# Sliding-window attention for one decoded token: another order of the steps between two units

## The chip, the cores and the metric

The kernel runs on one core of a Trainium2 chip. The metric is device time in microseconds of one execution; the time before is the median of three runs. All data are fp32.

## The reference, cut to what matters

```python
xn = layernorm(x)                                   # x [2, 1, 512]
q = (xn @ wq) -> [2, 32 heads, 128]                 # 8 key/value heads, 4 query heads share one
k, v = last 4096 rows of k_cache, v_cache           # [2, 8, 32768, 128] each
p = softmax(q @ k.T * 128**-0.5)                    # over the 4096 rows
s = (p @ v).reshape(2, 1, 4096) @ wo                # wo [4096, 512]
g = silu(gmlp(xn))                                  # w_in [512, 1792], w_out [896, 512]
out = x + s * g
```

The windows of keys and of values are 33.5 MB each, and each is read once; the weights are 22 MB.

## The kernel before, in words

**Units.** One unit is two key/value heads of one batch row: 4096 rows of keys and of values for each, 4.19 MB each way. There are eight units, four for each batch row. The keys of a unit lie in a slot as 64 blocks (J) of 128 partitions by 128, a half of the partitions for each head. They are worked on in four quarters (NCH) of 16 blocks.

**Steps of a unit.** Each is a function; the tile names are those of the profile.

- `turn(u, m)`: DVE turns quarter m of the keys within blocks of 32 by 32, `kt<-k`. Two buffers.
- `shares(u, m)`: PE multiplies the turned quarter by the queries, four column groups side by side, `sh<-kt,qbd` into one PSUM bank that all quarters share; ACT copies it out, `shs<-sh`. Two buffers for shs.
- `add_shares(u, m)`: PE adds the four partial sums over the head dimension, `s<-shs,add_dq`, into bank m of the score tile `s`. That tile has four banks and there is one of it for all units.
- `row_max`: DVE takes maxima of s, `m<-s`. `share_max`: small DVE steps `t` and `mg`, a PE product `mo<-mg,same` that spreads the maxima over the partitions, then `mx` and the exponent's bias `nb`.
- `probs`: ACT takes the exponent of all scores, `p<-s,nb`, with row sums `l`, in two instructions. `probs_t`: DVE turns p in two halves, `pT<-p`. `weights`: PE `mo<-l,heads` and the small DVE steps `ls` and `wd`, which make the scale.
- `values`: PE multiplies pT by the values, `acc<-v,pT`, 16 products that the profile shows as 32 matmuls. `scale_out`: ACT scales them, `o<-acc,wd`, four instructions. `collect`: PE puts o into the batch row's bank, `col<-o,sel`; for the last unit of a batch row DVE then reduces that bank to `oT`.

**Order.** PE, DVE, ACT and SP are wrapped so that each engine runs its instructions in the order in which the program issues them (`InOrder`, line 37: nearly every row of the profile has this line, and tiles tell the steps apart). The order of the loop body is therefore the order on each engine. What an instruction waits for is found from the tiles that it reads and writes.

**Loads.** SP issues all large loads: w_in, w_out, two halves of wq, then keys and values, then wo in pieces. They share four slots of 4.19 MB (`ring`); a load waits until the last reader of the slot that it takes is done, and all later loads wait behind it on SP. The order is k0, k1, v0, k2, v1, ..., k7, v6, v7. Readers that free a slot are the last turn of a unit's keys and the last product of its values.

**Before and behind the units.** A first stage makes the layer norm, the gMLP gate and the queries. Behind the units PE multiplies oT by wo (`part`, `so`), and the gate and x are applied.

Of the kernel before, what the change touches and what calls it, by code (L numbers as in the profile page):

```python
# [11 lines left out]
ALU = mybir.AluOpType  # L12
AX = mybir.AxisListType
# [8 lines left out]
def ap(t, offset, dims):  # L22

    return bass.AP(tensor=t.tensor, offset=t.offset + offset, ap=[list(t.ap[0])] + [list(d) for d in dims])
# [18 lines left out]
def kernel(  # L43
# [25 lines left out]
    NU = B * HKV // 2  # L69
    J = 2 * W // P  # L70
    JC = 512 // 32
    NCH = J // JC
# [7 lines left out]
    def slot(name):  # L80
        return ring.tile([P, SLOT], F32, tag="slot", name=name)
# [4 lines left out]
    def bank(name, tag):  # L86
        return ps.tile([P, 512], F32, tag=tag, name=name)
# [21 lines left out]
    def by_group(t, b, c0, c1):  # L109
        return bass.AP(tensor=t.tensor, offset=t.offset + b * D + c0, ap=[[DC, G], [1, c1 - c0]])  # L110

    def load_unit(cache, u, name):

        b, w = divmod(u, NU // B)
        t = slot(f"{name}{u}")
        first = cache[b, 2 * w, SK - W :, :]
        src = bass.AP(tensor=first.tensor, offset=first.offset, ap=[[SLOT, P // 2], [SK * DH, 2], [1, SLOT]])
        sp.dma_start(t, src)
        return t.rearrange("p (j d) -> p j d", d=DH)
# [163 lines left out]
    def q_of(u, dq):  # L283
        return ap(qbd, (u.n * 4 + dq) * 32, [[1, 32]])
# [5 lines left out]
    def turn(u, m):  # L290

        u.kt[m] = sb.tile([P, JC, DH], F32, tag="kt", name=f"kt{u.n}_{m}")
        dve.transpose(
            u.kt[m].rearrange("p j d -> p (j d)"), u.k[:, JC * m : JC * m + JC, :].rearrange("p j d -> p (j d)")
        )

    def shares(u, m):

        u.sh = bank(f"sh{u.n}_{m}", "sh")
        for dq in range(4):  # L300
            pe.matmul(
                u.sh[32 * dq : 32 * dq + 32, :], q_of(u, dq), u.kt[m][:, :, 32 * dq : 32 * dq + 32],
                start=True, stop=True,
            )
        u.shs[m] = sb.tile([P, 512], F32, tag="shs", name=f"shs{u.n}_{m}")
        act.activation(u.shs[m], u.sh, AF.Copy)

    def add_shares(u, m):
        if m == 0:
            u.s = ps.tile([P, NCH, 512], F32, tag="s", name=f"s{u.n}")  # L310
            u.m4 = sb.tile([P, 2, 2], F32, tag="m4", name=f"m4_{u.n}")
        pe.matmul(u.s[:, m, :], add_dq, u.shs[m], start=True, stop=True)

    def row_max(u, half):
        n = NCH // 2 * 512
        dve.tensor_reduce(
            u.m4[:, half, :], ap(u.s, half * n, [[1, 2], [2, n // 2]]), axis=AX.X, op=ALU.max
        )

    def share_max(u):  # L320
        t = sb.tile([P, 2], F32, tag="t", name=f"t{u.n}")
        dve.tensor_scalar_mul(t, u.m4[:, :, 0], am[:, 0:1])
        dve.scalar_tensor_tensor(t, u.m4[:, :, 1], am[:, 1:2], t, op0=ALU.mult, op1=ALU.add)
        mg = sb.tile([P, 2, G], F32, tag="mg", name=f"mg{u.n}")
        dve.tensor_mul(mg, ap(t, 0, [[1, 2], [0, G]]), ap(grpm, 0, [[0, 2], [1, G]]))
        u.mo = bank(f"mo{u.n}", "mo")
        pe.matmul(u.mo[:, : 2 * G], same, mg.rearrange("p a g -> p (a g)"), start=True, stop=True)
        mx = sb.tile([P, 1], F32, tag="mx", name=f"mx{u.n}")
        dve.reduce_max(mx, u.mo[:, : 2 * G], axis=AX.X)
        u.nb = sb.tile([P, 2], F32, tag="nb", name=f"nb{u.n}")  # L330
        dve.scalar_tensor_tensor(u.nb, ap(mx, 0, [[0, 2]]), -SCALE, negm, op0=ALU.mult, op1=ALU.add)

    def probs(u):

        u.p = sb.tile([P, J, 32], F32, tag="p", name=f"p{u.n}", bufs=1)
        u.l = sb.tile([P, 2], F32, tag="l", name=f"l{u.n}")
        for a in range(2):
            act.activation(
                ap(u.p, a, [[2, J * 16]]), ap(u.s, a, [[2, J * 16]]), AF.Exp,
                bias=u.nb[:, a : a + 1], scale=SCALE, accum_out=u.l[:, a : a + 1],  # L340
            )

    def probs_t(u, half):
        if half == 0:
            u.pT = sb.tile([P, J, 32], F32, tag="pT", name=f"pT{u.n}", bufs=1)
        h = slice(J // 2 * half, J // 2 * (half + 1))
        dve.transpose(u.pT[:, h].rearrange("p j r -> p (j r)"), u.p[:, h].rearrange("p j k -> p (j k)"))

    def weights(u):
        pe.matmul(u.mo[:, 2 * G : 2 * G + 2], heads, u.l, start=True, stop=True)  # L350
        l = sb.tile([P, 1], F32, tag="ls", name=f"ls{u.n}")
        dve.reduce_sum(l, u.mo[:, 2 * G : 2 * G + 2], axis=AX.X)
        dve.reciprocal(l, l)
        u.wd = sb.tile([P, 4], F32, tag="wd", name=f"wd{u.n}")
        dve.tensor_scalar_mul(u.wd, diag, l)

    def values(u):
        u.acc = bank(f"acc{u.n}", "acc")
        NQ = J // 4
        for q in range(NQ):  # L360
            c = q % G
            pe.matmul(
                u.acc[32 * c : 32 * c + 32, :], ap(u.pT, 4 * q * 32, [[4, 32]]),
                u.v[:, 4 * q : 4 * q + 4, :].rearrange("p j d -> p (j d)"), start=(q < G), stop=(q >= NQ - G),
            )

    def scale_out(u):
        u.o = sb.tile([P, 4, DH], F32, tag="o", name=f"o{u.n}")
        for jj in range(4):
            act.activation(  # L370
                u.o[:, jj, :], u.acc[:, jj * DH : (jj + 1) * DH], AF.Copy, scale=u.wd[:, jj : jj + 1]
            )
# [3 lines left out]
    def collect(u):  # L376
        if u.w == 0:
            col[u.b] = bank(f"col{u.b}", "col")[:, : 4 * 32].rearrange("p (j d) -> p j d", j=4)
        for e in range(4):
            pe.matmul(  # L380
                col[u.b][32 * u.w : 32 * u.w + 32], sel[:, 3 - e : 35 - e], u.o[:, :, 32 * e : 32 * e + 32],
                start=(e == 0), stop=(e == 3),
            )
        if u.w == NU // B - 1:
            dve.reduce_sum(oT[:, :, 16 * u.b], col[u.b].rearrange("p j d -> p d j"), axis=AX.X)

    units = []
    for n in range(NU):
        u = Unit()
# [1 line left out]
        u.b, u.w = divmod(n, NU // B)  # L391
        units.append(u)

    for n in range(NU + 1):
        if n < NU:
            units[n].k = load_unit(k_cache, n, "k")
        if n > 0:
            units[n - 1].v = load_unit(v_cache, n - 1, "v")

    wo_v = wo.rearrange("(p j) d -> p j d", j=32)  # L400
    blocks = []
# [2 lines left out]
    for i, piece in enumerate(pieces):  # L404
        t = slot(f"wo{i}").rearrange("p (j d) -> p j d", d=D)
        at = 0
        for n in piece:
# [3 lines left out]
            if j == 16:  # L411
                for b in range(B):
                    sp.dma_start(x4[16 * b : P : 32, :], by_group(x, b, 0, DC))

    prev = None
    for u in units:
        if prev is None:
            turn(u, 0)
            turn(u, 1)
        shares(u, 0)  # L420
        shares(u, 1)
        if prev is not None:
            scale_out(prev)
        add_shares(u, 0)
        turn(u, 2)
        shares(u, 2)
        add_shares(u, 1)
        turn(u, 3)
        shares(u, 3)
        add_shares(u, 2)  # L430
        if prev is not None:
            collect(prev)
        row_max(u, 0)
        add_shares(u, 3)
        row_max(u, 1)
        share_max(u)
        probs(u)
        nxt = units[u.n + 1] if u.n + 1 < NU else None
        if nxt is not None:
            turn(nxt, 0)  # L440
            turn(nxt, 1)
        probs_t(u, 0)
        probs_t(u, 1)
        weights(u)
        values(u)
        prev = u
    scale_out(prev)
    collect(prev)


    EARLY = 28
# [48 lines left out]
```

## Time and profile before

| | |
|---|---|
| three runs, median (lowest to highest) | 265.07 us (264.8 to 265.68) |
| the profiled execution, its own time | 264.93 us |
| its span in the profile | 263.1 us |
| busy PE / DVE / ACT / POOL | 160.1 / 136.1 / 54.8 / 2.5 us |
| granted TensorE clock, mean | 0.789 |
| DMA | 89.54 MB, mean 340 GB/s |

The span is what the trace covers; the profiled execution took 1.8 us more. All times inside a trace count from the span's start. A row of the view in order of time has the start in us, the duration, the engine, the line, the operation, out<-in by tile names, shapes and count, and in brackets the idle time before it and who ended it. Rows that follow closely are merged, so a row can stand for several instructions (x8). The page cuts the span into 40 slices; PEclk is the granted clock in tenths of full speed.

### The profile page before, as it was taken

Reading aid. Unit: us, or ns where it says so; the run is one execution under the profiler, and the core shown is the slowest. Engines: PE = TensorE matmul, PEld = TensorE weight load, DVE = VectorE, ACT = ScalarE, POOL = GpSimd, SP = SyncE. Lnnn points to the kernel's source line nnn. Section 1 sums busy time; section 2 is a strip of 40 time slices with the busy share of each in tenths; the row PEclk is TensorE's granted clock in tenths of the full one; section 3 lists DMA queues with packets and bytes.
Section 4 is the critical chain, followed back from the end, with each engine's and each line's share of the span. In section 5 each row is a group of like instructions: output and inputs, shape, how many; then the busy total and the mean of one; then the engine's idle time right before and its main releaser. Section 6 shows DMA issues by size and latency. Waiting matters only on the chain.

```text
span 263.1 us, 2303 instructions
## 1 busy us (share of the span) xinstructions
PE 160.1 (61%) x898; PEld 49.3 (19%) x898; DVE 136.1 (52%) x191; ACT 54.8 (21%) x109; POOL 2.5 (1%) x13
## 2 busy tenths in 40 slices
PE   0261893493299348926871884198438926872893
PEld 0111220021112112311221222122211212121141
DVE  3234116945916783576648364916692677545000
ACT  4014100020304111330313040305120430313100
POOL 3000000000000000000000000000000000000000
PEclk9996577577569858965995799569858975997698
DMA  7999999999999998997699399909992997591000
GB/s 280 427 450 438 438 412 453 408 438 433 428 446 408 463 408 354 453 399 323 239 418 458 162 398 399 473 5 398 403 466 90 418 458 323 209 376 53 0 2 1
DMA packets 3794, 89.54 MB, mean 340 GB/s; under 512 B 438, under 2 KB 454, under 8 KB 840
## 3 DMA queue, kind: packets, MB, share of 16 engines
q1 hardware_dynamic: 3768, 89.40, 80.6%
q8 instruction: 7, 0.11, 0.2%
q14 instruction: 3, 0.02, 0.0%
q10 hardware_dynamic: 16, 0.01, 0.0%
HBM read 89.40 MB, written 0.00 MB: 340 GB/s over the span
## 4 chain that ended last, share of the span: by engine, by line
PE 57%; DVE 31%; ACT 5%; DMA 4%; issue 2%; ACTq 0%; DVEq 0%
PE acc L37 17%; PE s L37 13%; PE sh L37 13%; DVE kt L37 13%; DVE m L37 7%; DMA win<-in_B_w_in_dram 4%; DVE pT L37 4%; PE q_ps L37 3%; PE part L37 2%; PE z L37 2%; ACT shs L37 2%; PE mo L37 2%; DVE t L37 1%; PE y L37 1%; ACT p L37 1%
## 5 line engine op out<-in xcount | busy, mean ns | idle before, releaser
L37 DVE STREAM_TRANSPOSE kt<-k 128x2048 f32<-128x2048 f32 x32 | 72.0, 2289 | 35.6 <-PE sh L37 35.6
L37 PE MATMUL acc<-v,pT 128*32 128x512 f32 x256 | 45.9, 880 | 18.0 <-DVE pT L37 18.0
L37 ACT ACTIVATE shs<-sh 128x512 f32<-128x512 f32 x32 | 19.1, 597 | 115.3 <-PE sh L37 115.3
L37 PE MATMUL sh<-kt,qbd 128*32 128x512 f32 x256 | 36.1, 639 | 10.3 <-ACT shs L37 6.2
L37 PE MATMUL s<-shs,add_dq 128*128 128x512 f32 x64 | 36.7, 656 | 5.6 <-DVE m L37 5.6
L37 DVE TENSOR_REDUCE m<-s 128x2 f32<-128x1024 f32 x16 | 19.6, 1224 | 29.3 <-PE s L37 29.3
L37 ACT ACTIVATE p<-s,nb 128x1024 f32<-128x1024 f32 x16 | 18.5, 1169 | 48.2 <-DVE nb L37 48.2
L37 DVE STREAM_TRANSPOSE pT<-p 128x1024 f32<-128x1024 f32 x16 | 18.7, 1205 | 2.5 <-ACT p L37 2.5
L37 PEld LDWEIGHTS acc<-v,pT 128*32 128x32 f32 x256 | 10.4, 158 | 46.8 <-issue 28.2
L37 PE MATMUL mo<-l,heads 128*128 128x2 f32 x16 | 4.7, 363 | 23.5 <-ACT p L37 23.5
L37 PEld LDWEIGHTS s<-shs,add_dq 128*128 128x128 f32 x64 | 9.7, 191 | 29.5 <-issue 29.5
L37 PE MATMUL mo<-mg,same 128*128 128x8 f32 x16 | 4.0, 321 | 16.3 <-DVE mg L37 16.3
L37 PEld LDWEIGHTS sh<-kt,qbd 128*32 128x32 f32 x256 | 5.8, 111 | 36.4 <-ACT shs L37 25.7
L37 ACT ACTIVATE o<-acc,wd 128x128 f32<-128x128 f32 x32 | 9.1, 373 | 7.5 <-PE acc L37 7.5
L37 PE MATMUL q_ps<-wq,xnT 128*32 128x512 f32 x64 | 9.3, 747 | 0.0
L37 PE MATMUL col<-o,sel 128*32 128x128 f32 x64 | 8.5, 276 | 1.3 <-ACT o L37 1.3
L37 PEld LDWEIGHTS mo<-l,heads 128*128 128x128 f32 x16 | 4.0, 311 | 24.2 <-ACT p L37 24.2
L37 PEld LDWEIGHTS col<-o,sel 128*32 128x32 f32 x64 | 6.3, 109 | 7.5 <-issue 5.3
L37 PEld LDWEIGHTS mo<-mg,same 128*128 128x128 f32 x16 | 3.2, 251 | 22.9 <-DVE mg L37 22.9
L37 PE MATMUL z<-win,xnT 128*32 128x448 f32 x32 | 4.8, 762 | 4.0 <-DMA win<-in_B_w_in_dram 4.0
L37 PE MATMUL part<-wo,oT 128*32 128x512 f32 x56 | 6.2, 593 | 0.4 <-issue 0.4
L37 PE MATMUL y<-wout,hT 128*32 128x512 f32 x14 | 3.6, 1059 | 4.0 <-DVE hT L37 4.0
(99 smaller groups left out, 57.8 us busy)
## 6 DMA issues: line engine op xcount, KB each, us to landing
k<-in_A_k_cache_dram SPq DMA_DIRECT2D x8, 4096.0 KB, 12.3
v<-in_A_v_cache_dram SPq DMA_DIRECT2D x8, 4096.0 KB, 18.0
wq<-in_A_wq_dram SPq DMA_DIRECT2D x2, 4096.0 KB, 29.4
wo<-in_A_wo_dram SPq DMA_DIRECT2D x1, 4096.0 KB
win<-in_B_w_in_dram SPq DMA_DIRECT2D x1, 3584.0 KB
wo<-in_A_wo_dram SPq DMA_DIRECT2D x1, 2048.0 KB
wout<-in_B_w_out_dram SPq DMA_DIRECT2D x1, 1792.0 KB, 15.0
wo<-in_A_wo_dram SPq DMA_DIRECT2D x1, 1024.0 KB
```

Of the source, the lines that this page charges most:

```text
L37: return self.tc.keep_in_program_order(call(*args, **kwargs))
```

## The change

The order of the loop body is written anew, and two other things go with it.

- Order. The exponent of the previous unit, `probs(prev)`, now opens the pass of a unit. Behind it come the turn and the shares of quarter 0, then the previous unit's `probs_t` and `weights`, the adding product of quarter 0, and the previous unit's `values`. Quarters 1 to 3 follow, each as turn, shares, add. Then come `scale_out` and `collect` of the previous unit, the maxima and `share_max`. The reduction to oT has its own step, `gather`, behind `share_max`.
- Maxima. The two instructions read quarters 0 to 2 and quarter 3, where they read two quarters each. Both stand behind the last `add_shares`.
- Loads. The order is k0, v0, k1, v1, ..., k7, v7.

```diff
-    def row_max(u, half):
-        n = NCH // 2 * 512
+    def row_max(u, i, c0, c1):
         dve.tensor_reduce(
-            u.m4[:, half, :], ap(u.s, half * n, [[1, 2], [2, n // 2]]), axis=AX.X, op=ALU.max
+            u.m4[:, i, :], ap(u.s, 512 * c0, [[1, 2], [2, 256 * (c1 - c0)]]), axis=AX.X, op=ALU.max
         )
...
+    def gather(u):
         if u.w == NU // B - 1:
             dve.reduce_sum(oT[:, :, 16 * u.b], col[u.b].rearrange("p j d -> p d j"), axis=AX.X)
...
-    for n in range(NU + 1):
-        if n < NU:
-            units[n].k = load_unit(k_cache, n, "k")
-        if n > 0:
-            units[n - 1].v = load_unit(v_cache, n - 1, "v")
+    for u in units:
+        u.k = load_unit(k_cache, u.n, "k")
+        u.v = load_unit(v_cache, u.n, "v")
...
+    def finish(u):
+        scale_out(u)
+        collect(u)
+
     prev = None
     for u in units:
-        if prev is None:
-            turn(u, 0)
-            turn(u, 1)
+        if prev is not None:
+            probs(prev)
+        turn(u, 0)
         shares(u, 0)
-        shares(u, 1)
         if prev is not None:
-            scale_out(prev)
+            probs_t(prev, 0)
+            probs_t(prev, 1)
+            weights(prev)
         add_shares(u, 0)
-        turn(u, 2)
-        shares(u, 2)
-        add_shares(u, 1)
-        turn(u, 3)
-        shares(u, 3)
-        add_shares(u, 2)
         if prev is not None:
-            collect(prev)
-        row_max(u, 0)
-        add_shares(u, 3)
-        row_max(u, 1)
+            values(prev)
+        for m in range(1, NCH):
+            turn(u, m)
+            shares(u, m)
+            add_shares(u, m)
+        if prev is not None:
+            finish(prev)
+        row_max(u, 0, 0, NCH - 1)
+        row_max(u, 1, NCH - 1, NCH)
         share_max(u)
-        probs(u)
-        nxt = units[u.n + 1] if u.n + 1 < NU else None
-        if nxt is not None:
-            turn(nxt, 0)
-            turn(nxt, 1)
-        probs_t(u, 0)
-        probs_t(u, 1)
-        weights(u)
-        values(u)
+        if prev is not None:
+            gather(prev)
         prev = u
-    scale_out(prev)
-    collect(prev)
+    probs(prev)
+    probs_t(prev, 0)
+    probs_t(prev, 1)
+    weights(prev)
+    values(prev)
+    finish(prev)
+    gather(prev)
```

## The prediction

> **What bounds the kernel now.** I read the page first (where the engines and the clock stand), then the order of time inside one unit, then the clock in small windows, then the instructions of the first unit.
>
> ```profile
> span 263.1 us, 2303 instructions
> ...
> PEclk9996577577569858965995799569858975997698
> ...
> GB/s 280 427 450 438 438 412 453 408 438 433 428 446 408 463 408 354 453 399 323 239 418 458 162 398 399 473 5 398 403 466 90 418 458 323 209 376 53 0 2 1
> ...
> PE 57%; DVE 31%; ACT 5%; DMA 4%; issue 2%; ACTq 0%; DVEq 0%
> ```
>
> A slice is 6.58 us. DMA carries 430 to 450 GB/s at first and then shows holes (162, 5, 90): from the middle on, loads wait for buffers. A unit brings 2 x 4.19 MB, 19.5 us at 430 GB/s. The chain of waits is PE and DVE in alternation. So what counts is the dependent chain of one unit. This is unit 2 with the end of unit 1, in the view in order of time:
>
> ```profile
> 101.91 1.03 PE L37 MATMUL sh<-kt,qbd 128*32 128x512 f32 x8
> 103.08 0.60 ACT L37 ACTIVATE shs<-sh 128x512 f32<-128x512 f32 x1 [9.89 <-PE sh L37]
> 103.72 1.06 PE L37 MATMUL sh<-kt,qbd 128*32 128x512 f32 x8 [0.79 <-ACT shs L37]
> 104.72 1.12 PE L37 MATMUL s<-shs,add_dq 128*128 128x512 f32 x2
> 104.92 0.60 ACT L37 ACTIVATE shs<-sh 128x512 f32<-128x512 f32 x1 [1.24 <-PE sh L37]
> 105.78 1.06 PE L37 MATMUL sh<-kt,qbd 128*32 128x512 f32 x8
> ...
> 108.82 1.13 PE L37 MATMUL s<-shs,add_dq 128*128 128x512 f32 x2
> 109.99 1.23 DVE L37 TENSOR_REDUCE m<-s 128x2 f32<-128x1024 f32 x1 [2.47 <-PE s L37]
> 111.36 1.10 PE L37 MATMUL s<-shs,add_dq 128*128 128x512 f32 x2 [0.42 <-DVE m L37]
> 112.49 1.22 DVE L37 TENSOR_REDUCE m<-s 128x2 f32<-128x1024 f32 x1 [1.28 <-PE s L37]
> 113.75 0.23 DVE L37 TENSOR_SCALAR t<-m,am 128x2 f32<-128x2 f32 x1
> ...
> 114.49 0.59 PE L37 MATMUL mo<-mg,same 128*128 128x8 f32 x2 [2.04 <-DVE mg L37]
> 115.33 0.16 DVE L37 SCALAR_TENSOR_TENSOR nb<-mx,negm 128x2 f32<-128x2 f32 x1
> 115.41 4.50 DVE L37 STREAM_TRANSPOSE kt<-k 128x2048 f32<-128x2048 f32 x2
> 115.58 1.18 ACT L37 ACTIVATE p<-s,nb 128x1024 f32<-128x1024 f32 x1 [5.96 <-DVE nb L37]
> 119.83 2.33 DVE L37 STREAM_TRANSPOSE pT<-p 128x1024 f32<-128x1024 f32 x2
> 121.08 5.35 PE L37 MATMUL acc<-v,pT 128*32 128x512 f32 x32 [2.46 <-DVE pT L37]
> 126.25 1.03 PE L37 MATMUL sh<-kt,qbd 128*32 128x512 f32 x8
> ```
>
> From one unit's first key product to the next is 24.34 us: 1.81 with an open copy (101.91 to 103.72), 6.16 for three pairs at 2.05 with the copy hidden, 3.87 for both maxima and the last adding product between them, 1.66 to the next turn, 4.42 for two turns, 1.25 for the first turned probabilities, 5.17 for the values. Two things are to be seen. The first maximum reads quarters 0 and 1 alone, yet starts when quarter 2 is added, and the last product waits for that maximum: waits go by the whole score tile, in program order. And PE is nearly idle from 112.5 to 121.1, which costs clock:
>
> ```profile
> 49.47:52.88 3.41, 2.69 (x16) 0.20 (x8) 3.41 (x2) 0.60 (x1) 0.00 (x0) 0.50 1.00 432
> 145.04:148.45 3.41, 3.02 (x16) 0.79 (x20) 1.90 (x5) 0.00 (x0) 0.00 (x0) 0.50 0.74 312
> 76.78:80.19 3.41, 2.62 (x25) 0.45 (x17) 1.76 (x1) 0.60 (x1) 0.00 (x0) 1.00 1.08 456
> 76.50:77.00 0.50, 0.50 (x8) 0.10 (x4) 0.00 (x0) 0.00 (x0) 0.00 (x0) 0.72 0.30 131
> 90.00:90.50 0.50, 0.30 (x2) 0.20 (x2) 0.17 (x1) 0.00 (x0) 0.00 (x0) 0.93 0.76 328
> 100.50:101.00 0.50, 0.50 (x8) 0.18 (x4) 0.00 (x0) 0.00 (x0) 0.00 (x0) 0.83 1.07 459
> ```
>
> (Busy windows: length, PE, PEld, DVE, ACT, POOL, granted clock, DMA.) A mean of 0.72, 0.93 and 0.83 over half a microsecond puts the changes of clock at 76.78, 90.43 and 100.67: 13.65 and 10.24 us apart, four and three steps of 3.41. PE goes up only behind a step that it filled: 3.02 of 3.41 busy was enough (the row from 145.04), 2.69 was not (from 49.47). At full clock a step with 2.62 busy stayed up (from 76.78). The Trainium skill, "TensorE: Matmul & The Clock Gate", Part 1, gives the same free-running window of 3.4 us with two rates; the trace agrees, with its 3.41.
>
> **The change, part by part.** Rows of the first unit, at half clock, and of one large group and one small:
>
> ```profile
> 46.32 6.70 DVE L37 STREAM_TRANSPOSE kt<-k 128x2048 f32<-128x2048 f32 x3
> 48.69 1.94 PE L37 MATMUL sh<-kt,qbd 128*32 128x512 f32 x8 [4.05 <-DVE kt L37]
> 50.69 0.60 ACT L37 ACTIVATE shs<-sh 128x512 f32<-128x512 f32 x1 [18.48 <-PE sh L37]
> 53.20 2.07 PE L37 MATMUL s<-shs,add_dq 128*128 128x512 f32 x2
> 63.70 0.23 DVE L37 TENSOR_SCALAR t<-m,am 128x2 f32<-128x2 f32 x1
> ...
> 96.29 5.79 PE L37 MATMUL acc<-v,pT 128*32 128x512 f32 x32 [2.46 <-DVE pT L37]
> 98.01 0.19 PEld L37 LDWEIGHTS acc<-v,pT 128*32 128x32 f32 x4 [0.66 <-issue]
> ...
> L37 DVE TENSOR_REDUCE oT<-col 128x32 f32<-128x128 f32 x2 | 0.6, 294 | 10.4 <-PE col L37 10.4
> ```
>
> *Quarters 1 to 3.* PE's order is now shares, add, shares, add of the same quarter, so each adding product waits for its own copy: 1.20 to the copy's start (103.72 to 104.92), 0.64 for the copy and its hand-over (103.08 to 103.72), 1.06 to the next product (104.72 to 105.78): 2.90 where 2.05 was. The turns (2.29 each) run ahead and are hidden. Two quarters, then 1.20 + 0.64 + 1.17 (108.82 to 109.99) up to the maximum: 8.81.
>
> *Maxima.* Both now stand behind the last adding product in program order, so by the whole-tile wait seen above the 3 + 1 split overlaps nothing. 1024 columns take 1.22 and 128 take 0.29, so 1.04 ns a column: 1.75 + 0.69 + 0.04 = 2.48 from the first to t. Scale-out and collect, now behind the last quarter, run beside the maxima on ACT and PE, which have nothing else until mo; were they longer than the 3.2 us that lie between, the rest would come on top.
>
> *Softmax.* t to the first turn stays 1.66 (113.75 to 115.41); turn to product 2.37 (46.32 to 48.69). The second turn and the turned probabilities, 2.2 + 1.25 on the old path, go behind the first product: p, two of 1.18, ends 0.3 after that product starts (115.58 + 2.4 against 115.41 + 2.37), and pT with its 2.33 ends 2.6 after it, before the adding product is through.
>
> *First quarter under the softmax.* It finds PE at half clock (idle from collect on for about 5 us): 2.00 to the copy (48.69 to 50.69), 0.65, 2.00 for the adding product (the 2.07 of the row at 53.20, less the overlap with the next): 4.65. The sums' small product (as long as the 0.59 at 114.49) fits into the copy's 0.65.
>
> *Values.* 32 matmuls in 8 groups of 0.85 (0.19 and 0.66 idle at 98.01) are 6.84 at half clock, 3.42 at full. If the clock rises w after the first product starts, a unit takes 8.81 + 2.48 + 1.66 + 2.37 + 4.65 + 3.42 + (w - 4.65)/2 = 23.39 + (w - 4.65)/2. Before, the stretch from 96.29 had its rise at 100.67 (w = 4.4); the shortest way is the 3.0 us of the row from 145.04, the longest two steps less the 0.39 us that may be missing, 6.4. So a unit takes 22.6 to 24.3 us. Seven steps are 23.9; a shorter unit moves its start forward against the steps, lengthens w and comes back to that. I take 23.85.
>
> *Loads.* v0 now goes second and k1 third, which enters its queue at the same place:
>
> ```profile
> 37.21 0.53 SPq L37 DMA_DIRECT2D v<-in_A_v_cache_dram  x1
> 77.32 1.03 PE L37 MATMUL sh<-kt,qbd 128*32 128x512 f32 x8
> 225.32 1.03 PE L37 MATMUL sh<-kt,qbd 128*32 128x512 f32 x8
> 237.17 0.23 DVE L37 TENSOR_SCALAR t<-m,am 128x2 f32<-128x2 f32 x1
> ```
>
> 26.5 MB stand in the queue up to its end; the slices reach that at about 64 us, and its turn is due near 69: hidden, 5 us to spare (each us beyond that costs one, once). Later keys wait for a unit's last turn, values for the value products, one after the other on SP; each is issued more than a unit's time before its use, and 19.5 us of transfer fit into 23.85.
>
> *First unit.* Its quarters now run at 4.65 cold. With copies open, a step holds about as little PE work as the one from 49.47 that did not raise the clock, so the rise comes a step later, at 59.7 instead of 56.3 (five and six steps ahead of 76.78): 4.65 + 4.65 + 3.7 + 3.0 = 16.0, then 2.48, so t stands at 67.2, not 63.7. The values then end near 79.6, where 77.32 stood: +2.3. All quarters cold would be 1.6 more; a rise one step earlier 1.7 less.
>
> *Sum.* 79.6 + 6 x 23.85 + 8.81 + 2.48 = 234.0 for the last unit's t, against 237.17; behind it the same steps follow. Before, the six units took (225.32 - 77.32)/6 = 24.67 each, of which one holds a gather. So -3.2 us: 264.93 in the profiled execution becomes 261.7. The median of the runs, 265.07, lies 0.14 above that execution; this is inside the rounding.
>
> **The rivals.**
> *The copy's gap keeps the clock down* (slower). Place: between the first product and its adding product, where only the small product of the sums runs. If that does not count as work, the step with the gap looks like the one of 2.69 of 3.41, and the rise waits for a step wholly behind the gap: w is 5.6 to 8.8, a unit 23.9 to 25.5, on average 24.7; with +2.3 at the start and -0.55 at the end (11.29 for 237.17 - 225.32) 267. It decides from a gap between 0.39 us (3.02 busy) and 0.72 (2.69). For it: the first unit's steps. Against it: 0.59 us of the small product stands in the gap.
> *The spaced quarters drop the clock.* Then each costs 4.65 and not 2.90, 5 us a unit, near 300. The row from 76.78 speaks against it: three quarters busy, clock 1.00. The Trainium skill, same page, "A second HAM failure mode: psum-queue depth-cycling", says that small idle times between groups of matmuls made the clock swing; that would give this case, and the trace so far does not bear it out.
> *No change.* Every open hand-over costs 0.2 us more than the rows (the adding product loads 128 columns of weights behind its wait, of which the trace shows no exposed case behind ACT): 0.8 a unit, and the gain is gone: 265.
> *The change does not do what it says, the good way:* the split maxima do overlap. Then 1.75 us of a unit goes, 250. The waits of the tile speak against it.
> *A lucky phase:* the first unit's clock rises a step earlier and the units stay below seven steps: 258.
>
> **How the numbers follow.** Forecast 0.64, with 259.8 to 263.5 as its own range; clock kept down 0.14; spaced quarters 0.03; no change 0.10; overlap 0.02; lucky phase 0.07. 0.3% (0.8 us) is about what a measurement of this kernel tells from no change. Faster: 0.64 + 0.02 + 0.07 and a third of the clock case where units stay near 23.9, 0.77. Same 0.09, slower 0.14. The range leaves out the overlap, the dropped clock, the worse half of the clock case and the better half of the lucky phase, 0.16 together; it takes the rest: 259.0 to 266.5.
>
> **What would show it.** In the changed profile: PE's idle before s with ACT shs as its releaser, about 0.7 each, four a unit; the quarters 2.9 apart; both maxima behind the last s, 1.75 and 0.69; the value products without a wait on pT; 23.9 us from unit to unit, and changes of the clock seven steps apart; k1's first turn waiting for nb, not for DMA. I am wrong if units take over 24.6, if the clock is 0.50 in quarters 1 to 3 of later units, or if the first maximum starts before the last s ends.

## The result, and the profile after

The changed kernel takes 262.41 us (median of 20 executions, 260.07 to 266.19), the kernel before 264.52 (20 executions beside them, 262.5 to 266.1). The ratio is 0.9874, 95% interval 0.9844 to 0.9904: 1.3% faster. The 20 executions of the changed kernel fall into two groups, 11 near 261 us and 9 near 265, and the ratio compares the first, to which the profiled execution (261.21 us) belongs, with all of the kernel before; the ratio of the plain medians is 0.992, and why the second group is longer was not profiled.

From the page after, the lines that answer to those of before: span, granted clock and DMA rate in 40 slices, and the chain that ended last by engine.

```profile
span 259.4 us, 2310 instructions
...
PEclk9996579569569967995998599779959995997798
...
GB/s 284 418 466 409 450 428 414 450 429 419 450 424 422 450 419 344 384 424 421 149 414 470 328 237 407 404 248 323 467 419 167 404 424 386 197 396 56 0 3 1
...
PE 53%; DVE 18%; DMA 16%; ACT 9%; issue 3%; ACTq 0%
```

The span is 3.7 us shorter, and the row of GB/s still has holes (149, 167): waiting work, not the loads, sets the end. On the chain DVE has gone from 31% to 18%, and ACT, the open copies, from 5% to 9%. DMA has gone from 4% to 16%, but nearly all of it lies before 47.02 us, where the chain now follows the load of k0 back; in the units no load is on it. The groups say the same of DVE and ACT (busy us, mean ns of one, then PE's idle time ahead of them and its releaser):

```profile
L37 PE MATMUL s<-shs,add_dq 128*128 128x512 f32 x64 | 43.6, 768 | 21.3 <-ACT shs L37 21.3
...
L37 PE MATMUL acc<-v,pT 128*32 128x512 f32 x256 | 35.8, 709 | 0.7 <-DVE pT L37 0.7
```

The wait on pT, which the product of values had in every unit before (2.46 in the rows shown), is gone but for 0.7 in the last unit. In its place the adding products wait 21.3 us for their copies. One unit in the order of time:

```profile
102.95 1.03 PE L37 MATMUL sh<-kt,qbd 128*32 128x512 f32 x8
104.77 1.13 PE L37 MATMUL s<-shs,add_dq 128*128 128x512 f32 x2 [0.79 <-ACT shs L37]
...
107.67 1.12 PE L37 MATMUL s<-shs,add_dq 128*128 128x512 f32 x2 [0.78 <-ACT shs L37]
...
110.56 1.12 PE L37 MATMUL s<-shs,add_dq 128*128 128x512 f32 x2 [0.78 <-ACT shs L37]
...
111.73 2.36 DVE L37 TENSOR_REDUCE m<-s 128x2 f32<-128x1536 f32 x2 [5.36 <-PE s L37]
114.12 0.23 DVE L37 TENSOR_SCALAR t<-m,am 128x2 f32<-128x2 f32 x1
...
115.56 2.30 DVE L37 STREAM_TRANSPOSE kt<-k 128x2048 f32<-128x2048 f32 x1
...
118.01 1.94 PE L37 MATMUL sh<-kt,qbd 128*32 128x512 f32 x8 [2.77 <-DVE kt L37]
...
119.88 0.59 PE L37 MATMUL mo<-l,heads 128*128 128x2 f32 x2
...
120.71 2.08 PE L37 MATMUL s<-shs,add_dq 128*128 128x512 f32 x2 [0.25 <-ACT shs L37]
...
122.72 4.30 PE L37 MATMUL acc<-v,pT 128*32 128x512 f32 x32
...
126.84 1.03 PE L37 MATMUL sh<-kt,qbd 128*32 128x512 f32 x8
```

From 102.95 to 126.84 are 23.89 us. The others, from the end of one unit's values to the next, take 23.89, 23.89, 23.99, 23.84 and 23.87. These are the same seven steps of the clock (busy windows: length, PE, PEld, DVE, ACT, POOL, granted clock, DMA):

```profile
117.26:120.67 3.41, 2.46 (x10) 0.74 (x10) 3.10 (x4) 1.47 (x3) 0.00 (x0) 0.50 0.98 423
120.67:124.09 3.42, 3.38 (x10) 0.91 (x14) 3.36 (x4) 0.00 (x0) 0.00 (x0) 0.50 1.07 462
124.09:127.50 3.41, 3.41 (x36) 0.97 (x28) 1.44 (x1) 0.00 (x0) 0.00 (x0) 1.00 0.02 5
127.50:130.91 3.41, 2.49 (x14) 0.45 (x10) 2.31 (x1) 0.60 (x2) 0.00 (x0) 1.00 0.85 308
130.91:134.33 3.42, 2.12 (x10) 0.46 (x10) 0.00 (x0) 1.12 (x3) 0.00 (x0) 1.00 1.07 460
134.33:137.74 3.41, 2.12 (x10) 1.09 (x10) 2.12 (x2) 1.11 (x5) 0.00 (x0) 1.00 1.04 452
137.74:141.16 3.42, 0.39 (x2) 0.30 (x2) 2.80 (x7) 1.53 (x3) 0.00 (x0) 1.00 0.87 374
```

Two steps of seven are at half clock; a full step (3.38 busy) brings the clock back at 124.09, a nearly empty one (0.39) costs it at 141.16. From the unit's first product at 118.01 to the rise are 6.08 us, the w of the prediction. In the seven units it is 6.07, 6.08, 6.08, 6.08, 5.88, 5.98 and 6.03.

The start and the last unit:

```profile
47.02 6.70 DVE L37 STREAM_TRANSPOSE kt<-k 128x2048 f32<-128x2048 f32 x3 [0.67 <-DMA k<-in_A_k_cache_dram]
...
54.10 1.90 PE L37 MATMUL sh<-kt,qbd 128*32 128x512 f32 x8
...
56.78 1.12 PE L37 MATMUL s<-shs,add_dq 128*128 128x512 f32 x2 [0.79 <-ACT shs L37]
...
66.14 0.23 DVE L37 TENSOR_SCALAR t<-m,am 128x2 f32<-128x2 f32 x1
...
67.78 2.30 DVE L37 STREAM_TRANSPOSE kt<-k 128x2048 f32<-128x2048 f32 x1
...
79.06 1.03 PE L37 MATMUL sh<-kt,qbd 128*32 128x512 f32 x8
...
222.44 1.03 PE L37 MATMUL sh<-kt,qbd 128*32 128x512 f32 x8
...
233.61 0.23 DVE L37 TENSOR_SCALAR t<-m,am 128x2 f32<-128x2 f32 x1
```

By these rows and those of before: the first unit's end, taken at the product behind its values, came 1.74 later (79.06 for 77.32); the six units to 222.44 saved 4.62 (143.38 for 148.00); the last unit to its t saved 0.68 (11.17 for 11.85). Together that is the -3.56 at t (233.61 for 237.17); behind t both kernels need nearly the same, 25.8 and 26.0.

### The profile page after: what moved, and what is told of

Same layout as the page of the kernel before. It is cut to its first block, busy times and chain, and to the rows that moved or that the text cites. A ratio compares the mean times of both kernels' runs of the same rounds, so it can differ in the third digit from the quotient of the medians.

```text
span 259.4 us, 2310 instructions
## 1 busy us (share of the span) xinstructions
PE 161.7 (62%) x898; PEld 49.2 (19%) x898; DVE 137.0 (53%) x191; ACT 54.8 (21%) x109; POOL 2.5 (1%) x13
## 4 chain that ended last, share of the span: by engine, by line
PE 53%; DVE 18%; DMA 16%; ACT 9%; issue 3%; ACTq 0%
PE s L37 17%; PE sh L37 16%; PE acc L37 14%; DMA k<-in_A_k_cache_dram 12%; ACT shs L37 7%; DVE m L37 7%; DVE kt L37 7%; DMA win<-in_B_w_in_dram 4%; PE part L37 2%; PE z L37 2%; DVE t L37 1%; PE mo L37 1%; ACT p L37 1%; DVE mg L37 1%; DVE mx L37 1%
## 5 line engine op out<-in xcount | busy, mean ns | idle before, releaser
L37 DVE STREAM_TRANSPOSE kt<-k 128x2048 f32<-128x2048 f32 x32 | 72.8, 2297 | 19.8 <-PE sh L37 19.1
L37 PE MATMUL s<-shs,add_dq 128*128 128x512 f32 x64 | 43.6, 768 | 21.3 <-ACT shs L37 21.3
L37 PE MATMUL sh<-kt,qbd 128*32 128x512 f32 x256 | 41.6, 729 | 24.3 <-DVE kt L37 24.3
L37 DVE TENSOR_REDUCE m<-s 128x2 f32<-128x1536 f32 (+1 forms) x16 | 18.8, 1219 | 42.9 <-PE s L37 42.9
L37 PE MATMUL acc<-v,pT 128*32 128x512 f32 x256 | 35.8, 709 | 0.7 <-DVE pT L37 0.7
L37 PEld LDWEIGHTS s<-shs,add_dq 128*128 128x128 f32 x64 | 11.1, 218 | 46.2 <-ACT shs L37 43.7
L37 PEld LDWEIGHTS acc<-v,pT 128*32 128x32 f32 x256 | 9.3, 146 | 30.8 <-issue 30.0
L37 PE MATMUL mo<-mg,same 128*128 128x8 f32 x16 | 3.3, 280 | 18.4 <-DVE mg L37 18.4
L37 PEld LDWEIGHTS mo<-mg,same 128*128 128x128 f32 x16 | 2.6, 203 | 21.1 <-DVE mg L37 21.1
```

The source lines that it names most:

```text
L37: return self.tc.keep_in_program_order(call(*args, **kwargs))
```

## The experiments

Two theories stood against each other. By mine the unit is held to seven steps of the clock, and the small product in the gap between the first product and its adding product counts as work. By the rival that product does not count: a step with the gap in it can't raise the clock. Both allow w = 6.07, so the result alone does not tell them apart. Times are medians of 4 executions (10 for the kernel before with the new loads), ratios are against the kernel before in the same round; "units" are the differences between the ends of the value products. Diffs are against the changed kernel unless another is named.

**A lag of half a microsecond**, and one of 1.1. A DVE maximum over part of the queries, into a tile that nobody reads, stands ahead of each unit's first turn (about 0.5 us in each of seven units).

```diff
             probs(prev)
+            lag = sb.tile([P, 1], F32, tag="lag", name=f"lag{u.n}")
+            dve.reduce_max(lag, qT[:, :400], axis=AX.X)      # second kernel: :1024
         turn(u, 0)
```

> The changed kernel with one more DVE instruction in every unit but the first, between the bias nb and the first turn: a maximum over 400 columns that nothing uses, about 0.50 us on the chain. My theory (a unit is held to seven steps of 3.41 us, 23.89; a later first product only shortens its time at half clock, from 6.0 to about 5.0 us): units stay at 23.9, the span at 259.4 within 1. Rival, the chain has a fixed length and seven steps are chance: units 24.4, the span 3.5 longer, about 263. Rival, the step that holds the copy's gap does not count as filled: the rise of the clock comes 8 or more us after the first product and units go over 25.

> The same with 1024 columns, about 1.14 us on the chain. My theory: half clock shrinks from 6.0 to 3.7 us behind the first product, units stay at 23.9, span 259.4 within 1. Fixed chain: units 25.0, span about 267. If the copy's gap keeps a step from counting, the first step to count starts 2.7 us or more behind the first product, the rise comes at about 7, and units take 25.5 or more, span about 271.

The short lag gave 268.81 us, ratio 1.0185 (1.0099 to 1.0271), span 267.9: slower than the kernel before. Units take 24.77, 24.33, 25.81, 24.96, 24.33, 25.81, with w 8.58, 6.86, 5.99, 8.97, 6.86, 5.99 and 8.97. So 3.5 us of lag in seven passes cost 8.5 us of span (8.4 from the first unit's t to the last one's). The long one gave 275.61, 1.0418 (1.0349 to 1.0487), span 274.4, units from 25.08 to 26.23. My theory's 259.4, expected for both, fell. The units of the rival, 25 and 25.5, are what the two lags gave on average (25.0 and 25.6). The order of time on PE in the short one, and two steps of its clock:

```profile
146.57 1.93 PE L37 MATMUL sh<-kt,qbd 128*32 128x512 f32 x8 [3.24 <-DVE kt L37]
148.44 0.59 PE L37 MATMUL mo<-l,heads 128*128 128x2 f32 x2
149.27 2.07 PE L37 MATMUL s<-shs,add_dq 128*128 128x512 f32 x2 [0.25 <-ACT shs L37]
151.27 5.74 PE L37 MATMUL acc<-v,pT 128*32 128x512 f32 x32
```

```profile
148.71:152.13 3.42, 3.17 (x8) 0.94 (x12) 3.00 (x5) 0.51 (x1) 0.00 (x0) 0.50 1.06 460
152.13:155.54 3.41, 3.41 (x20) 0.77 (x16) 1.96 (x1) 0.00 (x0) 0.00 (x0) 0.50 0.00 0
```

By its records the step from 148.71 is busy for 3.17 of 3.42 us, and the clock stays down for one more step. The step of the prediction that was busy for 3.02 raised it. The record of the small product has 0.32 us in this step (148.71 to 149.03): without it 2.85 are left. So the 0.59 us of that product seem to look busy in the records and not to count for the clock. Two steps of a later experiment (the first maximum ahead) agree: both are busy for 3.16 and hold the same gap of 0.25, but the first has 0.28 us of the small product, at 190.62, and did not raise the clock, while the second has 0.21, at 214.51, and did.

```profile
190.62:194.03 3.41, 3.16 (x11) 0.92 (x14) 3.34 (x6) 0.47 (x1) 0.00 (x0) 0.50 0.93 404
214.51:217.92 3.41, 3.16 (x11) 0.92 (x15) 3.34 (x6) 0.41 (x1) 0.00 (x0) 0.50 0.87 375
```

In the traces of all runs, from the first key product on, every cold step of the units with at most 2.88 us of other work kept the clock down, and every one with 2.95 or more raised it. One step does not fit: in the last unit of the short lag, where value products follow the small product, the clock rose behind 2.72 us, 2.69 of them value products. So 2.88 to 2.95 is where the edge lies for the work around the gap, and not for every product.

```profile
247.70:251.11 3.41, 2.72 (x17) 0.73 (x20) 2.23 (x5) 0.00 (x0) 0.00 (x0) 0.50 0.00 0
```

**The gap filled with work that counts.** Four products of 32 columns of ones by 128 columns of the queries, into an unused part of the mo bank, stand in the gap; the product of the sums moves behind the next shares and its small DVE steps (`scale`) behind the last turn. This with both lags.

```diff
+    def fill(u):
+        for g in range(G):
+            pe.matmul(u.mo[32 * g : 32 * g + 32, 64:192], ones[:, :32], qT[:, :128], start=True, stop=True)
...
             probs_t(prev, 1)
-            weights(prev)
+            fill(prev)
...
             turn(u, m)
+            if m == NCH - 1 and prev is not None:
+                scale(prev)
             shares(u, m)
+            if m == 1 and prev is not None:
+                weights(prev)
```

> The changed kernel with the 0.50 us lag of the first experiment, and the gap of the first copy filled with other work: four products of 32 by 128 columns that nobody reads stand there, and the product of the sums (two columns) goes into the copy of quarter 1, its small DVE steps behind the last turn. Theory now: a step with the gap did not count because the product of the sums is no work for the clock's meter; with real products in the gap it counts again, the rise comes 3.0 to 6.4 us behind the first product, and units are held to 23.9 at about 5.0; span about 259.5, where the lag alone gave 267.9. Rival, what stands in the gap does not matter (the meter wants a whole step without any wait): units 24.9, span 268.

> The same with the 1.14 us lag. Theory now: units still 23.9, the rise about 3.7 behind the first product; span about 259.5, where the lag alone gave 274.4. Rival as before: units 25.6, span 274. If the fill lengthens the path, a few tenths a unit on top, taken back by the clock.

With the short lag 261.79 us, 0.9859 (0.9802 to 0.9917), units 23.73 to 23.96, w mostly 4.71 to 5.06. With the long one 262.05, 0.9895 (0.982 to 0.997), units 24.34 falling to 23.87, w down to 3.6. The long lag cost 15 us of span without the fill (274.4 for 259.4) and 0.6 with it (260.0); from the first unit's t to the last one's, which leaves out the start, it is 12.7 and 1.6. The rows with the short lag, and the step ahead of the rise at 103.04:

```profile
98.33 1.94 PE L37 MATMUL sh<-kt,qbd 128*32 128x512 f32 x8 [3.24 <-DVE kt L37]
100.01 0.68 PE L37 MATMUL mo<-qT,ones 128*32 128x128 f32 x8
101.03 2.07 PE L37 MATMUL s<-shs,add_dq 128*128 128x512 f32 x2 [0.34 <-ACT shs L37]
103.03 3.67 PE L37 MATMUL acc<-v,pT 128*32 128x512 f32 x32
```

```profile
99.62:103.04 3.42, 3.08 (x16) 0.73 (x8) 3.42 (x3) 0.60 (x1) 0.00 (x0) 0.50 0.86 374
```

3.08 busy by the records, less than the 3.17 that did not do, raise the clock now. This shows both halves: the lock to seven steps, which swallows a lag of 0.5 us whole and one of 1.1 us but for the first few units, and the gap that decides whether the lock has room for it. The fill in the changed kernel without a lag was not run, so what it is worth by itself is not shown.

**The first maximum ahead of the last adding product**, alone and with the gap filled (the diff above):

```diff
             shares(u, m)
+            if m == NCH - 1:
+                row_max(u, 0, 0, NCH - 1)
             add_shares(u, m)
...
-        row_max(u, 0, 0, NCH - 1)
         row_max(u, 1, NCH - 1, NCH)
```

> The changed kernel with the maximum over quarters 0 to 2 issued ahead of the last adding product (products in the changed kernel's order). My theory: its 1.75 us go under the last quarter's product and copy (1.84 us), only the 0.69 of the last quarter stay behind the last product; units 1.6 us shorter before the clock's part, 20.8 to 22.5, span about 248, time about 251. Rival, the last product waits for that maximum as in the kernel before and nothing is won: units 23.9, time 262.

> The experiment with the first maximum ahead of the last adding product, with the gap filled as above. Theory now: that order's gain of 1.6 us a unit was eaten by the clock (half clock for 8.9 us behind the first product, units 23.8); with the gap filled the rise comes at 3.0 to 6.4, units 20.9 to 22.6, span about 245 where 257.0 stood. Rival, the last product waits for the maximum and the order gains nothing: units 23.5 or more, span 255 or more.

Alone 257.28 us, 0.97 (0.9617 to 0.9784); with the fill 244.0, 0.9208 (0.9148 to 0.9268), span 241.1. One unit of the first:

```profile
121.63 5.67 PE L37 MATMUL acc<-v,pT 128*32 128x512 f32 x32
...
134.91 1.10 PE L37 MATMUL s<-shs,add_dq 128*128 128x512 f32 x2 [0.95 <-DVE m L37]
```

The maximum now overlaps, and the last product waits 0.95 for it. But the units take 23.59, 23.74, 23.82, 23.96, 23.83, and only the sixth 22.16: w grows to 9.00 and the value products to 5.75 (5.67 in this row), until at the end w falls back to 5.65. For five units a chain shorter by 1.6 us is held to seven steps, as the prediction had it and my expectation for this run (20.8 to 22.5) did not. With the gap filled, w can't grow that far, and the units are 22.45, 21.06, 21.15, 22.64, 21.06, 21.15.

**Shares one quarter ahead** in quarters 1 to 3, the order of before, so that two copies are hidden again:

```diff
-        for m in range(1, NCH):
+        turn(u, 1)
+        shares(u, 1)
+        for m in range(2, NCH):
             turn(u, m)
             shares(u, m)
-            add_shares(u, m)
+            add_shares(u, m - 1)
+        add_shares(u, NCH - 1)
```

> The changed kernel with quarters 1 to 3 in the old order of products: the shares of the next quarter go ahead of the adding product, so that a copy runs under a product. My theory: from the first of these products to the maximum 7.1 us where 8.8 stood; the unit falls below seven steps and is no longer held, 20.7 to 22.4 us each, span about 247, time about 250. Rival, the turns or something else bound the quarters and the open copies cost nothing: units 23.9, time 262.

251.69 us, 0.9499 (0.9444 to 0.9554), span 249.0. The open copies of quarters 2 and 3 cost 0.85 each by the rows; 1.2 of these 1.7 us arrive (22.70 a unit on average: 23.20, 21.85, 22.87, 23.48, 21.89, 22.88), the rest goes into w, 5.77 to 8.64. I had expected 22.4 at most.

**PE kept busy in the softmax.** Four idle products a unit (ones by 448 columns of the queries, into the mo bank), two behind collect and two behind nb; then the same with the shares one quarter ahead, and the same kind in the kernel before (two behind the last adding product, four behind nb).

```diff
+    def keep(u, times):
+        for _ in range(times):
+            pe.matmul(u.mo[:, 64:512], ones, qT[:, :448], start=True, stop=True)
...
         dve.scalar_tensor_tensor(u.nb, ap(mx, 0, [[0, 2]]), -SCALE, negm, op0=ALU.mult, op1=ALU.add)
+        keep(u, 2)
...
         row_max(u, 1, NCH - 1, NCH)
+        u.mo = bank(f"mo{u.n}", "mo")
+        keep(u, 2)
         share_max(u)
```

> The changed kernel with four products of 448 columns in every unit that nobody reads (into unused columns of the bank of mo): two behind the last adding product, two behind the maxima. They keep PE at work where it stood still. My theory: the clock stays at 1.00 through the units, the first quarter and the values run at full clock, units 21.5, span about 243, time about 245. Rival, PE's clock is not what a unit loses (the added products delay mo or the first product instead): units 23.9 or more, time 262 to 266.

> Both: pairs of products and the four idle products. My theory: 21.5 less 1.7, 19.8 a unit, which is about what the loads take (two of 9.7 us): span 231 to 236, time 233 to 238, with loads among the releasers. Rival, loads bind earlier: units of 21 or more, time over 243.

> The kernel before with products of 448 columns that nobody reads, two behind the last adding product and four behind the maxima, so that PE does not stand still before the values. Theory: the old order loses 2.2 us a unit to half clock in the values and 0.2 in the product of the maxima; units 22.3 where 24.7 stood, span about 245. Against the changed order with the same cure (units 21.44, span 241.6) the new order is then worth 0.8 a unit without any part of the clock. Rival, the old order's chain does not feel the clock: 263.

In the changed kernel: 244.48 us, 0.9145 (0.907 to 0.9219), span 241.6, units 21.44 (one with a gather 21.64).

```profile
110.32 1.77 PE L37 MATMUL mo<-qT,ones 128*128 128x448 f32 x4 [0.26 <-DVE mx L37]
112.83 1.06 PE L37 MATMUL sh<-kt,qbd 128*32 128x512 f32 x8 [0.74 <-DVE kt L37]
...
115.72 3.67 PE L37 MATMUL acc<-v,pT 128*32 128x512 f32 x32
```

The first quarter takes 2.89 (112.83 to 115.72) where it took 4.71, and the values 3.67 for 4.30. So half clock cost the changed kernel 2.45 us a unit. With the shares ahead as well: 229.29 us, 0.8632 (0.8577 to 0.8687), the best version run here and ahead of both kernels; units 19.55. Its page:

```profile
span 229.1 us, 2437 instructions
...
PEclk9998578755597999999999999999999999999999
...
DMA  7999999999999999999999999999999999997000
```

The DMA row has no holes left. The loads (19.5 us for a unit, as the prediction worked it out) now take as long as the chain, but they do not yet bound it: against my expectation no step of the units waits for a load, and the chain from 91.9 to 111.5 is PE, DVE and ACT alone.

In the kernel before the cure took only half: 256.07, 0.9652 (0.9585 to 0.9719), units 23.72 to 23.98 where I had expected 22.3.

```profile
116.88 0.28 PE L37 MATMUL mo<-l,heads 128*128 128x2 f32 x2
119.50 5.12 PE L37 MATMUL acc<-v,pT 128*32 128x512 f32 x32 [2.35 <-DVE pT L37]
...
168.58 3.67 PE L37 MATMUL acc<-v,pT 128*32 128x512 f32 x32 [2.35 <-DVE pT L37]
```

```profile
115.70:119.11 3.41, 1.46 (x6) 0.76 (x4) 3.41 (x3) 0.74 (x2) 0.00 (x0) 1.00 1.03 444
119.11:122.53 3.42, 3.02 (x16) 0.80 (x20) 1.90 (x5) 0.00 (x0) 0.00 (x0) 0.50 0.96 412
```

The clock drops anyway, during the 2.35 us wait for pT, and the values take 5.12; only in two units, where the step lay otherwise, 3.67. What the new order is worth at full clock on both sides therefore stays open.

**Loads.** The old order in the changed kernel, and the new one in the kernel before.

```diff
-    for u in units:
-        u.k = load_unit(k_cache, u.n, "k")
-        u.v = load_unit(v_cache, u.n, "v")
+    for n in range(NU + 1):
+        if n < NU:
+            units[n].k = load_unit(k_cache, n, "k")
+        if n > 0:
+            units[n - 1].v = load_unit(v_cache, n - 1, "v")
```

> The changed kernel with the load order of the kernel before (k0, k1, v0, k2, v1, ...). My theory: no load is on a unit's chain, so units 23.9 and the span 259.4 within 1. Rival, the load order brings the gain: units back to 24.7, span about 263.

> The kernel before with the new load order alone (k0, v0, k1, v1, ...). My theory: span 263.1 within 1; k1 is now third in its queue and lands about when its turn is due, which may cost up to 0.7 once. Rival, the load order brings the gain: about 260.

260.8 us (0.9895, 0.983 to 0.996), span 259.3, units 23.89 as before; and 264.12 (0.9992, 0.9956 to 1.0029), span 263.5. The order of the loads is worth nothing here, either way.

## Why the prediction was right, and where its reasons were not

**The chain: right.** Quarters are 2.90 apart (104.77, 107.67, 110.56). Both maxima start behind the last adding product, 2.39 to t for the 2.48 forecast, and overlap nothing. From t to the turn are 1.44 where 1.66 was taken: that row was at half clock, and mo is now still at full clock (0.39 us for 0.59). Turn to product is 2.45 (2.37), the first quarter 4.71 (4.65), the values 4.12 up to the next product: 3.42 and 0.70 for the clock, as (w - 4.65)/2 gives with w = 6.07.

**The unit: right in value, by a bound that was partly wrong.** 23.9 us and seven steps came out as forecast (23.85). That a shorter unit comes back to them is shown by the early maximum, which gave back its 1.6 us to the clock. What failed is the premise that the small product fills the copy's gap as work, and with it the bounds of 3.0 and 6.4 for w. The rival's mechanism is the true one, nearly as it stood: a step counts only if it begins close to the adding product (0.46 us ahead of it did, at 214.51; 0.53 did not, at 190.62). The adding product starts 2.70 behind the first product, so w is at least 2.70 - 0.46 + 3.41 = 5.65 and at most a step more. Behind the first unit the shortest w in all runs of the changed order without a fill or idle products is 5.65, the longest 9.00, and my bounds hold only with the fill (3.6 to 6.3 in its units). The rival's time, 24.7 a unit and 267, did not come, because it took the mean over all phases; the chain of this kernel settles at w = 6.07, near the rival's best end. That it came out there is luck: the prediction's bounds say nothing of this edge. That w is 0.42 above the least, and in a locked unit a lag shortens it by twice its length, so by estimate 0.2 us more in the chain is enough to lose the lock. The half microsecond of the lag kernels showed the other side of that edge. So the sign was right with less room than 0.77 and 0.14 said.

**First unit: two errors that met.** "The rise comes a step later, at 59.7" was wrong: the second quarter's adding product already takes 1.12 at 56.78, the clock's records have the rise at 55.82, and t came 1.7 earlier for it. But k0 landed 0.7 later (47.02 for 46.32), and w, 6.07, was longer than the forecast's share for it: 79.1 where 79.6 stood. In the profiled execution with filled gap and short lag (264.32 us) the first unit ran cold into its fourth quarter (rise at 65.49, t at 70.12), about the "1.6 more" of the prediction, and the units behind it were no longer than elsewhere.

**Loads: right.** k1's first turn, at 67.78, waits for nb and not for its load, and the two runs with the load orders exchanged differ by nothing.

**Other rivals.** Spaced quarters do not drop the clock: with copies open and 2.12 of 3.41 us busy it stays at 1.00 (steps from 130.91 and 134.33). The swing that the Trainium skill, "TensorE: Matmul & The Clock Gate", "A second HAM failure mode: psum-queue depth-cycling", tells of does not appear here, at idle times of 0.78 us between groups. An open hand-over costs what the rows said, 0.78 of PE's idle time, and no 0.2 beyond.

## What to carry to other kernels

Before an edit on a chain that lets PE go cold, lay the chain on the clock's steps and ask which step raises the clock again and by how much it is filled: an edit of half a microsecond can be swallowed whole, or cost more than twice its length. A result that hits the number does not confirm the mechanism; a small lag put in on purpose shows on which side of an edge a kernel stands. Where PE has idle time within the chain, cheap work in it can be worth more than the reordering: four idle products a unit brought 7% here, the order itself 1.3%.

## What the runs showed of the hardware

- Records of PE are not the clock's measure of work. A product with two columns had a record of 0.59 us and did not count: 3.17 us of 3.42 with it did not raise the clock, 3.08 with products of 128 columns in its place did, and so did 3.02. Without the small product, steps with the gap or with key products stayed cold up to 2.88 and rose from 2.95; one step with 2.69 us of value products rose too, so the edge is not the same for all work.
- The clock falls without an idle step: a step with 1.46 of 3.41 us busy lost it (119.11 in the kernel before with idle products), and so did one with 1.58 in the kernel before (134.80), while 1.66 there (233.79) and 2.12 in the changed kernel kept it. The Trainium skill, "TensorE: Matmul & The Clock Gate", "Why this matters for your kernels", asks for gaps of no more than about 3 us between bursts. Here the clock fell at 119.11 with no gap over 2.35 us.
- A loop with one cold stretch locks to whole steps: units of 23.9 us are seven times 3.41, over changes of 1.1 us more (with the gap filled) and 1.6 us less in the chain. Where one unit does not fit, several lock together: with the long lag the rises come seven and eight steps apart in turn (two units, 51.2 us), with the early maximum and the fill six, six and seven (three units, 64.9 us).
